# The main rows of w_in by four GpSimd transfers over 128 partitions per group, in place of four SP transfers over 32

## The chip, the core and the metric

One Trainium2 chip, one of its cores. The metric is device time in microseconds (us); lower is better. PE is TensorE, PEld its weight load, DVE VectorE, ACT ScalarE, POOL GpSimd, SP SyncE. SP computes nothing here and issues most DMA transfers. POOL computes and issues some too: those of a queue of its own, called the software queue (q0 of the profile), while SP's go out on q1.

## The reference, cut to what matters

An mLSTM cell runs over a sequence, and its output goes through a feed-forward block with an `h * cos(h)` gate.

```python
batch, n_heads, seq, head_dim = (4, 8, 768, 40)
for t in range(S):
    m_new = np.maximum(f_gate[:, :, t] + m, i_gate[:, :, t])
    f_stab = np.exp(f_gate[:, :, t] + m - m_new)
    i_stab = np.exp(i_gate[:, :, t] - m_new)
    C = f_stab[..., None, None] * C + i_stab[..., None, None] * np.einsum('bhd,bhe->bhde', vt, kt)
    n = f_stab[:, :, None] * n + i_stab[:, :, None] * kt
    h_tilde = np.einsum('bhde,bhe->bhd', C, qt)
    denom = np.maximum(np.abs(np.einsum('bhd,bhd->bh', n, qt)[:, :, None]), 1.0)
    y[:, :, t] = sigmoid(o_gate[:, :, t]) * h_tilde / denom
...
x = y.transpose(0, 2, 1, 3).reshape(3072, 320)
h = x @ w_in                   # w_in  320 x 2048, float64
return (h * np.cos(h)) @ w_out # w_out 2048 x 320, float64
```

The two weight matrices come as 8-byte floats. The kernel reads them as pairs of 32-bit integers and makes 4-byte floats of them on the chip.

## The kernel before, in words

**Tiling.** The sequence is cut into 6 chunks of 128 steps; with 4 batches that makes 24 cells (n = 4 * chunk + batch). A cell builds scores of one chunk (`scores`, PE), weighs them with decay factors (`decay_exponents`, `decay`, `weigh`), multiplies by v (`values`), normalizes and turns the result into x transposed. Cells 0 to 3 are computed first (`first_cells`); from then on the feed-forward of chunk c runs on PE between the pieces of the cells of chunk c + 1. `first_period` is the first of these periods, with cell 4; `both_parts` are the others.

**Feed-forward.** `Up(c, f2)` multiplies 256 of the 2048 columns of w_in into two PSUM banks `pup` (lines 644 and 650); `near`, `rest`, `sin` and `gate` (lines 658 to 670, ACT and DVE in turn) make the gated tile `g`; `down` multiplies by w_out (line 682). The two `pup` banks are free again when `gate` has read them.

**Weights.** w_in has 320 rows, 40 for each of 8 heads. Of each head 32 rows are "main" rows, 8 are "low" rows. The main rows lie in `w_in_sb` as [128 partitions, 2, 2048]: partition 32a + d, index i, for row d of head 2a + i. The low rows lie in `w_in_l`. Both come in four groups f of 512 columns. `weights_in(f)` issues the transfers of a group and returns three pieces: main i = 0, main i = 1, and the low one. `weights_out(p)` issues one transfer for 256 rows of w_out, eight in all. Raw words land in tiles called `bits` and `low`; a piece is then made into floats by `take_apart` (two ACT instructions, lines 148 and 150), `bound` (two on DVE, 154 and 155) and `put_together` (one on DVE, 161, one on POOL, 162). Where the calls stand decides the place in each engine's order, since the program is scheduled by hand: every engine runs its instructions in the order in which the program writes them.

**Transfers of a group.** Four of SP, one for each a: 32 partitions, 2 rows of 4 KB for each, 256 KB. Then four more of SP for the low rows, 64 KB each. `bits` of w_in has two buffers, shared with the decay tile of cell 3.

**Order around the change.** In `first_cells`: SP loads for cells 2 and 3, then `weights_in(0)` (line 866), then loads for cells 4 and 5, w_out piece 0 (907), `weights_in(1)` (926), loads of E and o, w_out pieces 1 and 2 (945, 947), `weights_in(2)` (955). At the end of `first_period`: w_out piece 3, `weights_in(3)` (1022), w_out piece 4. POOL meanwhile masks decay tiles (line 392), multiplies k by weights (411), and does line 162; it issues DMAs at lines 223, 249, 262 and, for x of each later cell, 607. The first group's pieces are used at lines 922 to 942, the second's at 988 to 1004, w_out pieces 0 and 1 at 986 and 1006, `sigmoid(1)` and `decay(5)` follow at 1007 and 1008.

Of the kernel before, what the change touches and what calls it, by code (L numbers as in the profile page):

```python
# [12 lines left out]
I32 = mybir.dt.int32  # L13
# [16 lines left out]
def kernel(  # L30
# [20 lines left out]
    nc = tc.nc  # L51

    B, H, S, D = q.shape
# [3 lines left out]
    HP = H // 2  # L57
# [6 lines left out]
    NK = DM // 128  # L64
# [66 lines left out]

    WP, WQ = 512, 2 * DM
    w_out_bits = moe_w_out.bitcast(I32).rearrange("r (n two) -> r n two", two=2)
    w_in_heads = moe_w_in.bitcast(I32).rearrange("(a e d) m -> a d e m", e=NK, d=D)

    def to_float32(*made):
        for dst, bits in made:
            take_apart(dst, bits)
        for dst, bits in made:
            bound(dst)  # L140
        for dst, bits in made:
            put_together(dst, bits)

    def take_apart(dst, bits):
        n = dst.shape[1]
        hi, lo = bits[:, 0:n, 1], bits[:, 0:n, 0].bitcast(U32)

        nc.scalar.activation(out=dst, in_=hi.bitcast(FP), func=AF.Abs)

        nc.scalar.activation(out=bits[:, 0:n, 0], in_=lo, func=AF.Copy, scale=2.0 ** -29)  # L150

    def bound(dst):
        t = dst.bitcast(I32)
        nc.vector.tensor_scalar(out=dst, in0=dst, scalar1=LEAST, scalar2=GREATEST, op0=OP.max, op1=OP.min)
        nc.vector.tensor_scalar(out=t, in0=t, scalar1=5, scalar2=2, op0=OP.logical_shift_left,
                                op1=OP.logical_shift_right)

    def put_together(dst, bits):
        n = dst.shape[1]
        hi, t, m = bits[:, 0:n, 1], dst.bitcast(I32), bits[:, 0:n, 0]  # L160
        nc.vector.scalar_tensor_tensor(out=t, in0=hi, scalar=TOP2, in1=t, op0=OP.bitwise_and, op1=OP.bitwise_or)
        nc.gpsimd.tensor_tensor(out=t, in0=t, in1=m, op=OP.add)  # L162
# [3 lines left out]

    def weights_in(f):
        bits = pb.tile([128, NK, WP, 2], I32, name="bits", tag="bits")
        for a in range(HP):
            nc.sync.dma_start(out=bits[32 * a:32 * a + 32].rearrange("r i n two -> r i (n two)"),  # L170
                              in_=w_in_heads[a, 0:32, :, ts(f, 2 * WP)])
        low = p2.tile([128, 2 * 128, 2], I32, name="low", tag="S")
        for e in range(2):
            for a in range(2):
                nc.sync.dma_start(out=low[64 * e:64 * e + 64, ts(a, 128)].rearrange("r n two -> r (n two)"), in_=w_in_last[e, 2 * f + a])
        return [(w_in_sb[:, i, ts(f, WP)], bits[:, i]) for i in range(NK)] + [(w_in_l[:, ts(f, 2)].rearrange("p a n -> p (a n)"), low)]
# [80 lines left out]
    def gates_exp():  # L257
        for e in (eG, eW):
            nc.scalar.activation(out=e, in_=e, func=AF.Exp)
        dst = G_d.rearrange("(c j q) s -> j q c s", c=R, j=2)  # L260
        for j in range(2):
            nc.gpsimd.dma_start(out=dst[j], in_=eG[j:BH:2])
# [165 lines left out]
    def turn(n):  # L428

        pool, tag = psum(n)  # L430
        pts[n] = []
        for src in (qs(n), ks(n)):
            pt = pool.tile([128, HP, C], FP, name="pt", tag=tag)
            for p in range(HP):
                nc.tensor.transpose(pt[:, p], pair(src, p), ident)
            pts[n].append(pt)
        qkT[n] = [p1.tile([128, HP, C], FP, name=f"t{i}", tag=f"t{i}") for i in range(2)]
# [396 lines left out]
    def first_cells():  # L834
        nc.vector.memset(nil, 0.0)
        gates_in()
        nc.scalar.copy(out=ident_b, in_=ident)
        load(0, "qk")
        later_gates_in()
        load(0, "v")  # L840
        load(1, "qk")
        load_o(0, (0, 1))
        load(1, "v")
        load(2, "qk")
        load_E(0)
        load_E(1)
        warm(12)
        wall_in(0, 0, pmu)
        wall_in(0, 1, psum_o())
        gates_first()  # L850
        gates_first_out()
        spread(0, 0)
        decay_exponents_half(0, 0)
        turn(0)
        turn_out(0, False)
        gates_sums()
        spread(0, 1)
        decay_exponents_half(0, 1)
        decay(0)
        weigh_k(0)  # L860
        load_E(2)
        load(2, "v")
        load_E(3)
        load_o(0, (2, 3))
        load(3)
        pieces.extend(weights_in(0))
        wall_in(1, 0, psum_o())
        wall_in(1, 1, psum_o())
        gates_less_sums()
        spread(1, 0)  # L870
        decay_exponents_half(1, 0)
        scores(0)
        gates_maxima()
        turn(1)
        weigh(0)
        sigmoid(0, slice(0, 2))
        turn_out(1, False)
        spread(1, 1)
        decay_exponents_half(1, 1)
        gates_exponents()  # L880
        decay(1)
        weigh_k(1)
        values(0)
        normalize(0)
        scores(1)
        gates_exp()
        turn(2)
        turn_out(2, False)
        warm(2)
        seam(0)  # L890
        weigh(1)
        seam_out(0)
        state(0)
        load_two(B, "qk")
        decay_exponents(2)
        gates_diagonal()
        decay(2)
        weigh_k(2)
        values(1)
        load_E(B)  # L900
        normalize(1)
        scores(2)
        turn(3)
        sigmoid(0, slice(2, 4))
        seam(1)
        load_two(B, "Kv")
        outs.append((0, weights_out(0)))
        weigh(2)
        decay_exponents(3)
        turn_out(3)  # L910
        seam_out(1)
        values(2)
        decay(3)
        weigh_k(3)
        state(1)
        normalize(2)
        warm(2)
        scores(3)
        warm(1)
        seam(2)  # L920
        weigh(3)
        take_apart(*pieces[0])
        bound(pieces[0][0])
        put_together(*pieces.pop(0))
        values(3)
        pieces.extend(weights_in(1))
        seam_out(2)
        state(2)
        for piece in pieces[0:2]:
            take_apart(*piece)  # L930
        warm(3)
        pg = gates_turn()
        normalize(3)
        gates_keep(*pg)
        bound(pieces[0][0])
        put_together(*pieces.pop(0))
        warm(2)
        seam(3)
        seam_out(3)
        decay_exponents(B)  # L940
        bound(pieces[0][0])
        put_together(*pieces.pop(0))
        load_E(B + 1)
        load_o(1)
        outs.append((1, weights_out(1)))
        load_E(B + 2)
        outs.append((2, weights_out(2)))
        low_dimensions(B)
        turn_blocks(B)
        state(3)  # L950
        decay(B)
        weigh_k(B)
        odd_values(B)
        scale_q(B)
        ahead.append(weights_in(2))

    spot = const.tile([1, 1], FP, name="spot")
    nc.gpsimd.memset(spot, 0.0)
# [11 lines left out]
    def first_period():  # L970
        n = B
        up = Up(0, 0)
        scores(n)
        warm(8, psum_o())
        for e in range(2):
            up.near(e)
        weigh(n)
        for e in range(2):
            up.rest(e)
        clear_low()  # L980
        for e in range(2):
            up.sin(e)
            up.gate(e)
        values(n)
        seam(n)
        to_float32(outs.pop(0)[1])
        up = Up(0, 1)
        take_apart(*pieces[0])
        take_apart(*pieces[1])
        bound(pieces[0][0])  # L990
        put_together(*pieces[0])
        decay_exponents(n + 1)
        for e in range(2):
            up.near(e)
        for e in range(2):
            up.rest(e)
        take_apart(*pieces[2])
        bound(pieces[1][0])
        put_together(*pieces[1])
        for e in range(2):  # L1000
            up.sin(e)
            up.gate(e)
        bound(pieces[2][0])
        put_together(*pieces[2])
        pieces.clear()
        to_float32(outs.pop(0)[1])
        sigmoid(1)
        decay(n + 1)
        state(n)
        normalize_turned(n)  # L1010
        low_out(n)
        fade(n)
        turn_blocks(n + 1)
        scale_q(n + 1)
        weigh_k(n + 1)
        sin_next()
        down(0, 0)
        pieces.extend(ahead.pop(0))
        load_two((n + 3) // 2 * 2)
        load_E(n + 3)  # L1020
        outs.append((3, weights_out(3)))
        ahead.append(weights_in(3))
        outs.append((4, weights_out(4)))
# [102 lines left out]
    pieces, outs, ahead = [], [], []  # L1126
# [41 lines left out]
```

## Time and profile before

| | us |
|---|---|
| median of 3 runs | 534.6 (534.35 to 534.88) |
| the profiled execution | 531.87 |
| its span, first to last instruction | 530.1 |
| PE busy | 512.8 (97%) |
| DVE, ACT, POOL busy | 406.9, 286.6, 247.9 |
| w_in main transfers (line 170) | 16 of 256 KB, median 7.6 from issue to landing |
| w_out transfers (line 181) | 8 of 640 KB, 5.8 |
| x transfers of POOL (line 607) | 40 of 32 KB, 3.9 |
| q1, SP's queue | 55.64 MB of 57.81 MB |
| q0, POOL's queue | 1.49 MB |

Busy time is time in which an engine had an instruction under way. A timeline row gives start, length, engine, line, operation, tiles and in square brackets the idle time before it with the instruction that ended it. A row of the chain of waits gives start, length and the work, each step being what released the next one. A row of a table by stage gives the stretch and its length, then busy time and count of PE, PEld, DVE, ACT, POOL, then the granted share of PE's clock, the busy share of the 16 DMA engines, and GB/s.

### The profile page before, as it was taken

What the parts mean: (1) busy time and instruction counts of PE and PEld (TensorE: products, weight loads), DVE (VectorE), ACT (ScalarE), POOL (GpSimd) and SP (SyncE); (2) the same over time, 40 slices, a digit from 0 to 9 for tenths busy, and PEclk for the clock granted to TensorE, in tenths of its full rate; (3) what the DMA queues carried; (4) which work ended last, traced back from release to release, by engine and by line L of the source; (5) the groups of instructions that cost most, each with busy time, mean ns of one, the idle gap of its engine ahead of it and who ended that gap; (6) DMA issues with size and microseconds to landing.
All of it is one profiled execution on the core that took longest, in us unless ns stands there. A gap on an engine that the chain in (4) does not pass through costs nothing.

```text
span 530.1 us, 10427 instructions
## 1 busy us (share of the span) xinstructions
PE 512.8 (97%) x3848; PEld 346.9 (65%) x3848; DVE 406.9 (77%) x828; ACT 286.6 (54%) x546; POOL 247.9 (47%) x409
## 2 busy tenths in 40 slices
PE   7999779999999999999999999999999999999996
PEld 3875354556657666676677677677667676666765
DVE  4896798997778878888778888868898878664636
ACT  2896797857556537744547635537735531312221
POOL 7536454673775684554454554453433333121211
PEclk9999879999999999999999999999999999999999
DMA  9999999999339259149159149159110000000001
GB/s 139 227 183 213 231 195 231 246 238 208 48 118 196 56 109 181 41 120 170 56 116 157 42 113 176 49 116 160 47 56 6 1 6 6 26 25 1 1 0 50
DMA packets 97762, 57.81 MB, mean 109 GB/s; under 512 B 62048, under 2 KB 89792, under 8 KB 97712
## 3 DMA queue, kind: packets, MB, share of 16 engines
q1 hardware_dynamic: 96240, 55.64, 51.1%
q0 software_dynamic: 1424, 1.49, 1.4%
q8 instruction: 30, 0.49, 0.4%
q14 instruction: 20, 0.16, 0.1%
q10 hardware_dynamic: 48, 0.02, 0.0%
HBM read 51.71 MB, written 4.11 MB: 105 GB/s over the span
## 4 chain that ended last, share of the span: by engine, by line
PE 81%; DVE 7%; DMA 6%; POOL 1%; issue 1%; SPq 1%; ACT 1%; DVEq 0%; POOLq 0%
PE pup L650 26%; PE acc L760 25%; PE pup L644 8%; PE ps L475 4%; PE po L682 3%; PE late L760 3%; DMA bits<-in_moe_w_in_dram 3%; PE vt L510 2%; PE vt L501 2%; PE pu L601 2%; DMA o<-in_o_gate_dram 1%; PE pw L832 1%; DVE t L456 1%; PE ph L491 1%; DMA bits<-in_moe_w_out_dram 1%
## 5 line engine op out<-in xcount | busy, mean ns | idle before, releaser
L650 PE MATMUL pup<-xT,w_in_sb 128*128 128x512 f32 x384 | 176.7, 603 | 3.1 <-DVE g L670 2.9
L658 ACT ACTIVATE n<-pup 128x512 int32<-128x512 f32 x96 | 54.0, 595 | 193.6 <-PE pup L644 141.6
L650 PEld LDWEIGHTS pup<-xT,w_in_sb 128*128 128x128 f32 x384 | 70.4, 191 | 90.3 <-issue 88.0
L661 DVE SCALAR_TENSOR_TENSOR n<-pup,n 128x512 f32<-128x512 f32 x96 | 63.0, 687 | 82.3 <-ACT n L658 80.9
L724 POOL TENSOR_TENSOR D<-g 128x128 f32<-128x128 f32 x40 | 19.7, 492 | 145.6 <-DVE g L670 145.6
L666 ACT ACTIVATE n<-n 128x512 f32<-128x512 f32 x96 | 59.3, 631 | 16.1 <-DVE n L661 16.1
L670 DVE SCALAR_TENSOR_TENSOR g<-pup,n 128x512 f32<-128x512 f32 x96 | 61.9, 684 | 2.2 <-ACT n L666 1.4
L760 PE MATMUL acc<-w_out_sb,g 128*128 128x160 f32 x320 | 58.6, 304 | 0.0
L760 PE MATMUL acc<-T,g 128*128 128x160 f32 x320 | 58.0, 301 | 0.1
L644 PE MATMUL pup<-xL,w_in_l 64*128 64x512 f32 x192 | 55.2, 650 | 0.9 <-POOL w_in_l L162 0.9
L607 POOL DMA_DIRECT2D xL<-xT x40 | 22.5, 563 | 65.1 <-DVE xT L538 61.6
L760 PEld LDWEIGHTS acc<-w_out_sb,g 128*128 128x128 f32 x320 | 47.8, 190 | 5.6 <-issue 4.2
L760 PEld LDWEIGHTS acc<-T,g 128*128 128x128 f32 x320 | 48.1, 190 | 3.7 <-issue 3.0
L406 ACT ACTIVATE E<-E,tab 128x128 f32<-128x128 f32 x160 | 49.0, 389 | 0.2
L682 PE MATMUL po<-w_out_sb,g 128*128 128x320 f32 x128 | 36.2, 436 | 0.0
L760 PE MATMUL acc<-T,S 128*128 128x160 f32 x160 | 35.0, 300 | 0.0
L475 PEld LDWEIGHTS ps<-t,t 40*128 40x128 f32 (+1 forms) x384 | 24.2, 187 | 12.6 <-DVE t L456 7.5
L682 PEld LDWEIGHTS po<-w_out_sb,g 128*128 128x128 f32 x128 | 24.0, 190 | 11.9 <-issue 1.9
L481 DVE TENSOR_TENSOR E<-ps,E 128x512 f32<-128x512 f32 x48 | 30.7, 680 | 1.4 <-PE ps L475 1.3
L644 PEld LDWEIGHTS pup<-xL,w_in_l 64*128 64x128 f32 x192 | 14.8, 187 | 24.0 <-issue 19.6
L760 PE MATMUL acc<-w_out_sb,S 128*128 128x160 f32 x160 | 28.8, 299 | 0.0
L962 ACT ACT_TABLE_LOAD x22 | 28.2, 1283 | 0.4
(178 smaller groups left out, 878.0 us busy)
## 6 DMA issues: line engine op xcount, KB each, us to landing
E<-M_d SPq DMA_DIRECT2D x22, 512.0 KB, 4.3
qr<-in_q_dram SPq DMA_DIRECT2D x36, 160.0 KB, 3.1
kr<-in_k_dram SPq DMA_DIRECT2D x36, 160.0 KB, 5.4
G<-G_d SPq DMA_DIRECT2D x20, 256.0 KB, 5.2
bits<-in_moe_w_out_dram SPq DMA_DIRECT2D x8, 640.0 KB, 5.8
bits<-in_moe_w_in_dram SPq DMA_DIRECT2D x16, 256.0 KB, 7.6
out_dram<-o_sb SPq DMA_DIRECT2D x24, 160.0 KB, 1.9
ks<-in_k_dram SPq DMA_DIRECT2D x10, 320.0 KB, 7.5
```

What stands on the lines that cost most here:

```text
L406: nc.scalar.activation(out=Es[n][:, h], in_=Es[n][:, h], func=AF.Exp, scale=-1.0, bias=tab[:, c, 0, g:g + 1])
L475: nc.tensor.matmul(ps[j][:, p], kT[r, p], qT[r, p], start=True, stop=True)
L481: nc.vector.tensor_tensor(out=w, in0=pss[n][j], in1=w, op=OP.mult)
L644: nc.tensor.matmul(pu, w_in_l[r, f2], xL[c][r].rearrange("p b t -> p (b t)"), start=ahead, stop=not ahead)
L650: nc.tensor.matmul(pu.rearrange("p (b t) -> p b t", b=B), w_in_sb[:, i, ts(2 * f2 + e, 128)], xT[c][:, i:NK * B:NK], start=(i == 0 and not ...
L658: nc.scalar.activation(out=self.n[e], in_=self.pu[e], func=AF.Copy, bias=0.25)
L661: nc.vector.scalar_tensor_tensor(out=self.n[e].bitcast(FP), in0=self.pu[e], scalar=0.25, in1=self.n[e], op0=OP.add, op1=OP.subtract)
L666: nc.scalar.activation(out=r, in_=r, func=AF.Sin, scale=TWO_PI_DOWN)
L670: nc.vector.scalar_tensor_tensor(out=g, in0=self.pu[e], scalar=TWO_PI, in1=self.n[e].bitcast(FP), op0=OP.mult, op1=OP.mult)
L682: nc.tensor.matmul(po[c][b], gs[c, f][:, ts(b, C)], w_out_sb[:, f], start=(f == 0), stop=(f == NF - 1))
L760: nc.tensor.matmul(a, lhs, rhs, start=start, stop=stop)
L962: nc.scalar.activation(out=spot, in_=spot, func=AF.Sin)
```

## The change

The main rows of a group are issued by POOL, and cut another way: one transfer for each index i and each half x of the 512 columns, over all 128 partitions, 2 KB for each, again 256 KB. The source is viewed as [i][a][d][column], so that a transfer walks four heads of 32 rows. The low rows stay on SP. Two calls of `weights_in` move with all their eight transfers: that of group 0 goes behind `gates_exp()` (which ends with two DMAs of POOL), that of group 2 from the end of `first_cells` into `first_period`, behind the making of w_out piece 0. Groups 1 and 3 stay where they were.

```diff
-    w_in_heads = moe_w_in.bitcast(I32).rearrange("(a e d) m -> a d e m", e=NK, d=D)
+    w_in_heads = moe_w_in.bitcast(I32).rearrange("(a e d) m -> e a d m", e=NK, d=D)
...
         bits = pb.tile([128, NK, WP, 2], I32, name="bits", tag="bits")
-        for a in range(HP):
-            nc.sync.dma_start(out=bits[32 * a:32 * a + 32].rearrange("r i n two -> r i (n two)"),
-                              in_=w_in_heads[a, 0:32, :, ts(f, 2 * WP)])
+        for i in range(NK):
+            for x in range(2):
+                nc.gpsimd.dma_start(out=bits[:, i, ts(x, WP // 2)].rearrange("r n two -> r (n two)"),
+                                    in_=w_in_heads[i, :, 0:32, ts(2 * f + x, WP)])
...
         load(3)
-        pieces.extend(weights_in(0))
         wall_in(1, 0, psum_o())
...
         gates_exp()
+        pieces.extend(weights_in(0))
         turn(2)
...
         scale_q(B)
-        ahead.append(weights_in(2))
...
         to_float32(outs.pop(0)[1])
+        ahead.append(weights_in(2))
         up = Up(0, 1)
```

## The prediction

> **What bounds the kernel now.** I read the slices of the page first, then PE's timeline, then the chain of waits between 42 and 76 us, then the tables by stage.
>
> ```profile
> PE   7999779999999999999999999999999999999996
> PEclk9999879999999999999999999999999999999999
> DMA  9999999999339259149159149159110000000001
> 60.54 5.34 PE L650 MATMUL pup<-xT,w_in_sb 128*128 128x512 f32 x8 [2.89 <-DVE g L670]
> 75.32 0.65 PE L501 MATMUL vt<-E,vs 128*32 128x128 f32 x8 [2.79 <-DVE E L481]
> ```
>
> PE is full but for slices 5 and 6 (53 to 80 us), where its clock drops as well; the DMA engines are full for 12 slices. So a transfer can move the end only before about 80 us; behind that PE runs nearly without a gap, and what it has gained or lost there reaches the end whole. PE's two holes there, 2.89 and 2.79 us, are the only long ones past the start. The table by stage has what they cost:
>
> ```profile
> 44.00:46.00 2.00, 2.00 (x18) 1.03 (x14) 1.34 (x3) 1.81 (x3) 2.00 (x4) 1.00 1.04 362
> 46.00:49.00 3.00, 3.00 (x77) 2.33 (x76) 2.89 (x5) 2.42 (x4) 2.01 (x2) 1.00 1.03 214
> 60.50:63.90 3.40, 3.36 (x4) 1.51 (x5) 2.78 (x6) 2.02 (x3) 1.46 (x2) 0.50 1.00 289
> 75.30:80.90 5.60, 5.58 (x76) 3.95 (x76) 5.46 (x10) 5.57 (x13) 2.85 (x3) 0.50 1.31 164
> ```
>
> After each hole PE runs at half clock (0.50), for 3.4 and 5.6 us, which costs 1.7 and 2.8 us more. The upper two rows serve below: 44 to 46 us is w_out traffic over 128 partitions, 362 GB/s; 46 to 49 us is w_in over 32 partitions, 214 GB/s, with the DMA engines equally busy (1.04, 1.03). The chain says what ends last:
>
> ```profile
> 42.95 6.57 DMA bits<-in_moe_w_in_dram
> ...
> 49.54 7.59 DMA o<-in_o_gate_dram
> ...
> 57.15 4.69 DMA bits<-in_moe_w_out_dram
> ...
> 61.86 0.79 ACT w_out_sb L148
> ...
> 75.32 0.65 PE vt L501 x8
> ```
>
> SP's transfers follow each other: group 1 of w_in, the o gate, w_out piece 1. ACT stands in order before the last, and from its start (61.86) a chain of ACT and DVE work (w_out piece 1, sigmoid, decay of cell 5, `near`, `weigh`) leads to PE's values of cell 5 (75.32): 13.46 us with hardly a gap. The earlier hole comes from ACT too:
>
> ```profile
> 53.53 0.66 ACT L148 ACTIVATE w_in_sb<-bits 128x512 f32<-128x512 f32 x1 [4.33 <-DMA bits<-in_moe_w_in_dram]
> ```
>
> ACT waits 4.33 us for group 1, so `near`, `rest`, `sin` and `gate` of Up(0, 1) are late, and PE waits for the PSUM banks.
>
> **Part 1: what POOL pays.** Each group costs POOL four issues. POOL's nearest rows:
>
> ```profile
> L607 POOL DMA_DIRECT2D xL<-xT x40: 545/565/634, 69.5 to 444.5; - x40
> L249 POOL DMA_DIRECT2D M_d<-kr x1: 645/645/645, 17.0 to 17.0; - x1
> 21.63 1.11 POOL L262 DMA_DIRECT2D G_d<-kr  x2
> 24.17 1.09 POOL L392 TENSOR_SCALAR_AFFINE_SELECT E<-E 128x1024 f32<-128x1024 f32 x1 [1.43 <-DVE E L391]
> 25.30 1.06 ACT L402 ACTIVATE E<-E 128x1024 f32<-128x1024 f32 x1 [0.89 <-POOL E L392]
> ```
>
> 64 rows take 0.565, 160 rows 0.645 us; for 128 rows I take 0.6, so 2.4 us for a group (bounds 0.545 and, as the one copy that shares POOL's time with DVE at its worst, line 162's 1.75, that is 2.2 to 7.0).
> Group 0: POOL is free of G_d at 22.74 and issues until 25.15; the mask of cell 2 behind it starts 0.97 us later than 24.17, since 1.43 of the 2.4 was idle. ACT's decay of cell 2 had waited for that mask, so it is 0.97 later, then sigmoid, copies and the decay of cell 3; `weigh(3)` on DVE and PE's values of cell 3 (33.08) come 0.8 later.
> Group 1: behind line 162 of piece 0, at 36.9 to 39.3 with that 0.8 in it; the next POOL work waits for DVE until 39.0, so 0.3 us late, and PE reaches the second half of Up(0, 0) at 41.1, when it is made (40.6). Nothing.
> Group 2: at about 53.0 to 55.4, behind line 162 of w_out piece 0; piece 0 of group 1 is then put together by 56.7, and PE wants it at 58.5. Nothing; without that cover each 0.1 us per issue would cost 0.4.
> Group 3: before the mask of cell 6 (74.39), which ACT reads at 78.36. Nothing.
>
> **Part 2: what SP and the DMA engines get.** SP loses 16 issues (0.43 us each in the median) and goes on at once to what stood behind. The bytes stay. A group is 1.05 MB: 4.9 us at 214 GB/s, 2.9 at 362. The first is the row of the old shape (4 KB in 32 partitions), the second that of w_out (2560 B in 128), nearest to the new one; I take the second, so 2.0 us saved per group, bounds 0 and 2.0. No row shows a big transfer of POOL's beside SP's; the small xL took 1.7 to 8.1 us to land, in the busy stages like SP's own, so I let both queues share in order of issue.
> Group 0 lands near 32 (ACT takes it at 33.3 now). Group 1 is issued 4 to 6 us earlier than SP's 42.55; it and w_out piece 0 are both in by 48 to 50, where ACT wants them at 48.5 and 50.0. The 4.33 us are gone. The loads of k and v for cell 4 share the engines with it, which can hold PE's values of cell 4 back by up to 1.5 us (46.3 before); that is absorbed below.
>
> **Part 3: the sum.** Without the wait, with 0.8 of shift, ACT is through `sin` of Up(0, 1) at 57.0; the gate's first bank is free about 58.3, PE finishes `down(0, 0)` at 58.5. The first hole and its half clock go: Up(0, 2) ends at 63.1 and not 66.9. But the second chain then decides: values of cell 5 start 13.46 us after ACT begins w_out piece 1, so the gain is 61.86 less the later of 57.0 and that landing. The landing was at 61.84. To its credit: two groups of w_in faster (4.0, bounds 0 and 4.0), and some 1 us of engine time lost between 53 and 59, where the eight o transfers crept out (DMA share 0.84 there). To its debit: group 2, issued from 53 now, where SP issued it at 60.0, behind that piece: 0 to 4.9, I take half of 2.9. So 61.84 - 4.0 - 1.0 + 1.5 = 58.4, bounds 57.0 and 65.7. Gain 61.86 - 58.4 = 3.4 us, PE's shift of 0.8 contained in it. The second hole and its half clock stay, since PE is early and waits for the same chain. Against the profiled execution 531.87 (span 530.1 and 1.8 around it) that is 528.5; the median stands 2.7 above that execution, so 534.6 - 3.4 = **531.2 us**. With the landing between 57.0 and 60.7 it is 529.8 to 533.5.
>
> A rule that speaks against the change: the rows
>
> ```profile
> 84.22 1.15 POOL L607 DMA_DIRECT2D xL<-xT  x2 [2.71 <-DVE xT L538]
> 84.29 0.43 DVE L155 TENSOR_SCALAR w_in_sb<-w_in_sb 128x512 int32<-128x512 int32 x1
> ```
>
> show two issues of POOL in 1.15 us while DVE ran its quick 0.43 us form. The Trainium skill (SBUF — State Buffer, "SBUF: two separate sides") holds that such a DVE instruction locks GpSimd out of writing descriptors and names 0.62 us becoming 3.1. By that figure a group would take 12.4 us and the kernel about 540 us; these rows do not agree with it.
>
> **Rivals.**
> *Second hole gone too.* If PE's hole before cell 5's values (about 2.5 us) no longer drops the clock, 2.8 more: 528.4. For: the first hole's half clock began only after nearly all of 57.5 to 60.5 was idle. Against: the second dropped it with 2.79. Chance 0.12.
> *Cancelled.* The new shape is no faster (214 GB/s) and the chain gets its piece at 61.84 - 1 + 1.5, so 62.3: 535.0. For: the engines are busy either way. Chance 0.13.
> *Slower, in the DMA queue.* Group 2 goes wholly ahead of w_out piece 1 at the old rate: 61.84 - 1.0 + 4.9 = 65.7, 3.9 us late, 538.5. It decides from the point where what group 2 takes exceeds what groups 0 and 1 save. For: the piece is SP's ninth to tenth behind low rows and o. Against: SP reaches it sooner. Chance 0.13.
> *Slower, on POOL.* An issue over 1.8 us each: then 4 x 1.8 - 1.43 = 5.8 us of shift takes ACT past 61.86, and more counts in full; at 2.5 us each 3 us, 537.6. Against: 44 issues between 0.53 and 0.66. Chance 0.07.
> *Few engines.* The new transfer lands late because it runs on a part of the 16 DMA engines. If all four of a group share 4 engines, 128 packets follow each other on each; at the software queue's 0.138 us (median of its 2 KB packets) 17.7 us, group 0 lands at 43 and ACT stands from 33.3: 10 us, 545. For: the source has 4 outermost rows. Against: POOL's transfers here all landed on 16. Chance 0.07.
> The Trainium skill (DMA: Bandwidth & Descriptors, "Why a DMA increments its semaphore by 16 and not by 1") gives that rule: the slowest dimension of both sides sets the engines, so 4 here, and for GpSimd a rotating start, under which the four transfers would fill 16 and nothing be lost. No run so far shows it.
>
> **From cases to numbers.** Forecast 0.48, then as given. Faster (forecast's, and the second hole) 0.59; within 0.2%, about 1.1 us and what a measurement here can tell, 0.14; slower 0.27. Range 528.2 to 538.5: all but the tails of the first and the dearest cases.
>
> **What would show it.** POOL's four issues near 0.6 us each; the mask of cell 2 at 25.1; no wait of ACT for `bits` at 50; PE's hole before Up(0, 2) gone and its clock whole from 60 to 64; ACT's line 148 of w_out piece 1 near 58.4 and values of cell 5 near 71.9. GB/s while w_in flows tells the shape's worth. I am wrong if w_out piece 1 lands after 61.8, if ACT waits at 33 for group 0, or if POOL blocks.

## The result, and the profile after

The changed kernel takes 542.04 us (median of 4 runs, 541.34 to 542.95) beside 534.48 us for the kernel before on the same chip: ratio 1.0152, interval 1.0134 to 1.017. It is slower, by 8.1 us with this ratio; 531.2 was forecast. The profiled execution is the one of 541.34 us, its span 539.5 against 530.1.

The slices of the page, PE, its clock and the DMA engines, 13.5 us to a slice:

```profile
PE   7996969799999999999999999999999999999995
PEclk9999979999999999999999999999999999999998
DMA  9899999799626637429338329349220000000001
bits<-in_moe_w_in_dram POOLq DMA_DIRECT2D x16, 256.0 KB, 10.4
```

PE's fourth, sixth and eighth digits (40.5 to 54, 67 to 81 and 94 to 108 us) are lower than their neighbours, the clock falls in the sixth, and behind the eighth PE is as full as before. The last line is from the table of DMA issues: a transfer of the new kind needs 10.4 us in the median from issue to landing; SP's needed 7.6. The timelines of POOL, PE with one line of DVE, and ACT show what was lost (start, length, engine, line, what, in brackets the idle time before it and what ended that):

```profile
21.93 2.76 POOL L171 DMA_DIRECT2D bits<-in_moe_w_in_dram  x4
24.70 1.10 POOL L393 TENSOR_SCALAR_AFFINE_SELECT E<-E 128x1024 f32<-128x1024 f32 x1
36.73 2.98 POOL L171 DMA_DIRECT2D bits<-in_moe_w_in_dram  x4
50.54 0.31 POOL L418 COPY vr<-vs 128x128 f32<-128x128 f32 x1 [5.02 <-DMA vs<-in_v_dram]
57.75 2.71 POOL L171 DMA_DIRECT2D bits<-in_moe_w_in_dram  x4
82.00 3.03 POOL L171 DMA_DIRECT2D bits<-in_moe_w_in_dram  x4
```

```profile
50.62 0.43 PE L502 MATMUL vt<-E,vs 128*32 128x128 f32 x8 [2.92 <-DMA vs<-in_v_dram]
64.79 3.67 PE L651 MATMUL pup<-xT,w_in_sb 128*128 128x512 f32 x8
74.20 7.11 PE L683 MATMUL po<-w_out_sb,g 128*128 128x320 f32 x16 [4.68 <-POOL w_out_sb L162]
83.33 0.43 PE L502 MATMUL vt<-E,vs 128*32 128x128 f32 x8 [0.94 <-DVE E L482]
97.44 3.67 PE L651 MATMUL pup<-xT,w_in_sb 128*128 128x512 f32 x8 [2.19 <-DVE g L671]
85.36 1.26 DVE L155 TENSOR_SCALAR w_out_sb<-w_out_sb 128x640 int32<-128x640 int32 x1
```

```profile
52.70 0.81 ACT L148 ACTIVATE w_out_sb<-bits 128x640 f32<-128x640 f32 x1 [3.56 <-DMA bits<-in_moe_w_out_dram]
54.09 0.67 ACT L148 ACTIVATE w_in_sb<-bits 128x512 f32<-128x512 f32 x1
69.76 0.78 ACT L148 ACTIVATE w_out_sb<-bits 128x640 f32<-128x640 f32 x1 [7.10 <-DMA bits<-in_moe_w_out_dram]
```

The two waits that the change removes are gone: ACT no longer waits for group 1 of w_in (second line of the last fence, 4.33 us before), and Up(0, 2) begins behind `down(0, 0)` without a hole (second line of PE's). But Up(0, 2) begins at 64.79 where it began at 60.54, and three waits are new or longer, all for transfers of **SP**: v of cell 4 (PE and POOL, 50.5), w_out piece 0 (52.70), w_out piece 1 (69.76; 7.10 us, before 3.28).

Values of cell 5 begin at 83.33 instead of 75.32, 8.0 us late, as does the weighing on DVE that they wait for. PE's wait there is short (0.94 us, before 2.79), and PE runs at full clock behind it, so that its next multiplication of main rows into `pup` begins only 5.5 us late (86.60, before 81.14). That is lost again on DVE: its lines 154 and 155 behind the weighing take 1.1 us longer (the last one 1.26 us, before 0.50), while POOL, idle there before, issues group 3 and masks. PE then waits 2.19 us for the gate at 97.44. Values of cell 6 begin at 109.37 instead of 100.20, 9.2 of the 9.4 us by which the span grew. The loads of cells 6 and 7 are late too (v lands at 89.95, before at 82.22), but the trace shows no wait for them.

The chain of waits between 15 and 90 us names the same (start, length):

```profile
38.35 1.98 SPq L346
40.39 8.58 SPq L182
...
58.64 11.11 DMA bits<-in_moe_w_out_dram
69.76 0.05 ACT w_out_sb L148
83.33 0.43 PE vt L502 x8
```

SP itself stood for 8.58 us in the issue of w_out piece 0 (2.11 before), behind v's load, so its whole queue is late. Then piece 1, issued at 58.64 (57.15 before), flies for 11.11 us (4.69 before). The share of the two queues while v should have come, 42 to 45 us, first in the changed kernel, then in the kernel before (packets, MB, share of 16 engines):

```profile
q0 software_dynamic: 292, 0.56, 102.7%
q14 instruction: 1, 0.01, 1.0%
q1 hardware_dynamic: 1, 0.00, 0.1%
```

```profile
q1 hardware_dynamic: 1339, 0.69, 98.7%
```

q0 is POOL's queue, q1 SP's. For 3 us the engines serve only group 1; SP's queue moves one packet. In the trace v's packets begin at 45, though SP was through with issuing them at 40.34, and v lands at 50.49 instead of 44.09.

### The profile page after: what moved, and what is told of

Read it like the earlier page. It is cut to its first block, busy times and chain, and to the rows that moved or that the text cites. A ratio compares the mean times of both kernels' runs of the same rounds, so it can differ in the third digit from the quotient of the medians.

```text
span 539.5 us, 10425 instructions
## 1 busy us (share of the span) xinstructions
PE 513.3 (95%) x3848; PEld 346.5 (64%) x3848; DVE 412.4 (76%) x828; ACT 286.4 (53%) x546; POOL 259.5 (48%) x425
## 4 chain that ended last, share of the span: by engine, by line
PE 77%; DMA 6%; DVE 6%; SPq 4%; ACT 4%; issue 1%; POOL 1%; DVEq 0%; ACTq 0%
PE pup L651 25%; PE acc L761 24%; PE pup L645 8%; PE ps L476 3%; PE po L683 3%; PE late L761 3%; PE vt L511 2%; DMA bits<-in_moe_w_out_dram 2%; PE vt L502 2%; DMA low<-in_moe_w_in_dram 2%; SPq L182 2%; PE pu L602 1%; DMA E<-M_d 1%; DVE t L457 1%; PE pw L833 1%
## 5 line engine op out<-in xcount | busy, mean ns | idle before, releaser
L683 PE MATMUL po<-w_out_sb,g 128*128 128x320 f32 x128 | 38.8, 459 | 5.1 <-POOL w_out_sb L162 5.1
L683 PEld LDWEIGHTS po<-w_out_sb,g 128*128 128x128 f32 x128 | 25.4, 202 | 18.4 <-POOL w_out_sb L162 6.7
L645 PEld LDWEIGHTS pup<-xL,w_in_l 64*128 64x128 f32 x192 | 14.4, 184 | 25.0 <-issue 19.6
## 6 DMA issues: line engine op xcount, KB each, us to landing
bits<-in_moe_w_in_dram POOLq DMA_DIRECT2D x16, 256.0 KB, 10.4
```

The costliest lines, as they stand in the source:

```text
L645: nc.tensor.matmul(pu, w_in_l[r, f2], xL[c][r].rearrange("p b t -> p (b t)"), start=ahead, stop=not ahead)
L683: nc.tensor.matmul(po[c][b], gs[c, f][:, ts(b, C)], w_out_sb[:, f], start=(f == 0), stop=(f == NF - 1))
```

## The experiments

Three theories were told apart. **Few engines**: the cut is what costs, because a transfer of the new shape keeps its data on a part of the DMA engines. **Collision**: any second queue that carries a megabyte takes the engines away from SP's transfers, which are due earlier. **POOL**: the issues cost POOL's own time. Some expectations call them A, B and C. Besides, the forecast's gain itself was tested. Ratios are to the kernel before on the same chip.

| run | w_in's main rows | median us | ratio (interval) |
|---|---|---|---|
| e1_pool_rows32 | all by POOL, old cut | 539.44 | 1.0111 (1.0063 to 1.0159) |
| e4_g2_sp | group 2 by SP | 540.81 | 1.0112 (1.0064 to 1.0161) |
| e5_g12_sp | groups 1, 2 by SP | 539.48 | 1.0099 (1.0064 to 1.0134) |
| e8_swap | kernel before, w_out piece 1 a little earlier | 534.6 | 1.0002 (0.9978 to 1.0026) |
| e6_g0_only | group 0 by POOL | 532.61 | 0.9991 (0.9974 to 1.0008) |
| e6_g1_only | group 1 by POOL | 539.03 | 1.0122 (1.0103 to 1.0141) |
| e6_g2_only | group 2 by POOL | 542.9 | 1.018 (1.0154 to 1.0205) |
| e6_g3_only | group 3 by POOL | 537.84 | 1.0089 (1.0064 to 1.0114) |
| e7_late | all by POOL, issued later | 551.42 | 1.0359 (1.0326 to 1.0393) |
| e2_sp_cols | all by SP, new cut | 554.73 | 1.0411 (1.0387 to 1.0434) |
| e10_words | by SP; POOL issues words | 534.0 | 1.0017 (1.0002 to 1.0033) |
| e9_early | kernel before, w_out piece 1 much earlier | 533.53 | 0.9998 (0.9983 to 1.0013) |

**The queue without the cut.** The changed kernel with the old view of w_in and

```diff
-        for i in range(NK):
-            for x in range(2):
-                nc.gpsimd.dma_start(out=bits[:, i, ts(x, WP // 2)].rearrange("r n two -> r (n two)"),
-                                    in_=w_in_heads[i, :, 0:32, ts(2 * f + x, WP)])
+        for a in range(HP):
+            nc.gpsimd.dma_start(out=bits[32 * a:32 * a + 32].rearrange("r i n two -> r i (n two)"),
+                                in_=w_in_heads[a, 0:32, :, ts(f, 2 * WP)])
```

> POOL still issues four transfers per group at the changed kernel's places, but in the old cut: 32 partitions, 2 rows of 4 KB each, so that the outermost dimension of both sides is 32. Theory A (few engines: the changed cut puts each transfer's data on 4 of the 16 DMA engines, and SP's transfers, which need all 16, wait for those): the group spreads over 16 engines, lands within some 6 us of its issue in the middle stages, w_out piece 1 lands by 62 us and not at 69.74, and the time comes back to 532 to 536 us. Theory B (any second queue with this traffic takes the engines from SP's, whatever the cut): w_out piece 1 still lands at 68 to 70 us and the time stays at 540 to 543. Theory C (POOL's own time, 2.7 to 3.0 us per group): 540 to 543 as well, with the landings early.

Measured: 1.0111. SP's issue of w_out piece 0, PE at its values of cell 4, and ACT at w_out piece 1:

```profile
40.70 9.28 SPq L181 DMA_DIRECT2D bits<-in_moe_w_out_dram  x1
52.20 0.66 PE L501 MATMUL vt<-E,vs 128*32 128x128 f32 x8 [5.25 <-DMA vs<-in_v_dram]
66.45 0.81 ACT L148 ACTIVATE w_out_sb<-bits 128x640 f32<-128x640 f32 x1 [2.51 <-DMA bits<-in_moe_w_out_dram]
```

v of cell 4 lands at 52.06, later than in the changed kernel: the collision is there without the new cut. Piece 1 flies for 6.65 us, not 11.1, and lands at 66.43, between the 62 of theory A and the 68 to 70 of theory B; the time lies between theirs as well. So the cut is part of what group 2 does to piece 1. As times the two kernels can't be told apart, their intervals overlap.

**The cut without the queue.** The changed kernel with one word changed back:

```diff
-                nc.gpsimd.dma_start(out=bits[:, i, ts(x, WP // 2)].rearrange("r n two -> r (n two)"),
+                nc.sync.dma_start(out=bits[:, i, ts(x, WP // 2)].rearrange("r n two -> r (n two)"),
```

> The new cut (four transfers over 128 partitions a group) at the changed kernel's places, but issued by SP: one queue, in order. If the cut is what costs (few-engines theory), group 1 lands later than the 53.43 of the kernel before, or the transfers behind it do, and the time is 539 to 543 as in the changed kernel. If the second queue is what costs (collision theory), k and v of cell 4 land by 44 and w_out piece 1 by 63, as before, and the time is 533 to 537; up to 537 because a transfer whose data lies on four engines keeps the transfers behind it on those engines waiting.

Measured: 1.0411, the slowest of all, outside what either theory gave. Two stretches of it in which such a group flows, by windows (window, its length, busy time of PE, PEld, DVE, ACT, POOL, then granted clock, share of the DMA engines, GB/s):

```profile
25.00:28.00 3.00, 3.00 (x48) 2.65 (x47) 2.90 (x9) 2.95 (x4) 0.74 (x1) 1.00 0.27 94
53.00:56.00 3.00, 3.00 (x69) 1.98 (x62) 2.84 (x5) 1.51 (x2) 1.98 (x2) 1.00 0.26 89
```

A quarter of the engines is busy and 89 to 94 GB/s flow, where the old shape had all of them and 214. The four transfers of group 0 land one after another, at 28.06, 31.14, 34.99 and 38.32. So on SP's queue the few-engines theory holds in full; and as the cut alone costs so much there, this run does not tell what the second queue costs. By POOL the same shape was not so slow: group 0 of the changed kernel lands at 28.39, 30.24, 32.23 and 33.52, and its queue alone moved 205 GB/s at 27 us.

**Group by group.** One group by POOL in the new cut, the others by SP in the old cut, all at the changed kernel's places (here for group 1):

```diff
+        if f != 1:
+            for a in range(HP):
+                nc.sync.dma_start(out=bits[32 * a:32 * a + 32].rearrange("r i n two -> r i (n two)"),
+                                  in_=w_in_rows[a, 0:32, :, ts(f, 2 * WP)])
+        else:
+            for i in range(NK):
...
```

> Group 0 alone by POOL in the new cut, at the changed kernel's place. Here SP's queue has only the 160-byte loads and small ones beside it, and nothing of the trace of the changed kernel up to 36 us is late. Collision theory and POOL theory both: 533 to 536 (at most 1.3 us for the mask of cell 2). If it gives over 537, the start has a price that the traces do not show.

> Group 1 alone goes by POOL in the new cut, at the place of the changed kernel; the others go by SP in the old cut at that kernel's places. Collision theory: v of cell 4 lands 4 to 7 us later than the 44.09 of the kernel before, w_out piece 1 is issued 1 to 2 us later and lands near 63 with its short flight of about 4.5 us, values of cell 5 near 77 (before 75.32), and the time is 1.5 to 3 us over the kernel before. Few-engines theory (the cut is what costs): the same delay, because this run has the cut, so it does not tell them apart; POOL theory: 2.7 to 3.0 us of POOL's time for four issues, which shows as a wait for POOL somewhere between 37 and 50 us, and the time is up to 3 us over with v of cell 4 landing as before.

> Group 2 alone by POOL in the new cut, at the place of the changed kernel. Up to 57 us this is the kernel before. Collision theory: w_out piece 1 is issued near 57.2 and lands 8 to 11 us later (66 to 68) where before it took 4.7 us, values of cell 5 begin near 80 to 82, and the time is 3 to 6 us over the kernel before, the largest of the three single groups. If the first hole of the tensor engine going away were worth its time, as predicted, the time would be 3 us under.

> Group 3 alone by POOL in the new cut, at the place of the changed kernel. Up to 75 us this is the kernel before. Collision theory: v and k of cells 6 and 7 land some 7 us later than the 82.22 of the kernel before, holes ahead of the values of cells 6 and 7, and the time is 1.5 to 5 us over. The run with groups 0 and 3 by POOL gave 5.5 us over, so if groups 0 and 3 are told apart this run gives near 5 and group 0 near nothing; if it gives under 2, group 0 has a price that the trace did not show.

Group 0 costs nothing that can be measured, each of the others alone 0.9 to 1.8%: 6.5, 9.6 and 4.7 us for groups 1, 2 and 3 by these ratios. For groups 1 and 2 that is more than the 1.5 to 3 and 3 to 6 us expected. SP's issues and PE with group 1 alone, then with group 2 alone, then PE with group 3 alone:

```profile
33.82 8.01 SPq L352 DMA_DIRECT2D vs<-in_v_dram  x1
41.89 10.19 SPq L188 DMA_DIRECT2D bits<-in_moe_w_out_dram  x1
53.61 0.65 PE L508 MATMUL vt<-E,vs 128*32 128x128 f32 x8 [6.89 <-DMA vs<-in_v_dram]
80.81 0.43 PE L508 MATMUL vt<-E,vs 128*32 128x128 f32 x8 [2.03 <-DVE E L488]
```

```profile
59.30 0.68 SPq L188 DMA_DIRECT2D bits<-in_moe_w_out_dram  x1
74.75 7.47 PE L689 MATMUL po<-w_out_sb,g 128*128 128x320 f32 x16 [5.85 <-POOL w_out_sb L163]
84.25 0.43 PE L508 MATMUL vt<-E,vs 128*32 128x128 f32 x8 [0.94 <-DVE E L488]
```

```profile
95.83 2.08 PE L651 MATMUL pup<-xL,w_in_l 64*128 64x512 f32 x4 [3.73 <-POOL w_in_l L163]
```

Each group hits the SP transfer that was in flight or next when it was issued. Group 1 hits v of cell 4 (and here, issued at 35.67 and not 36.73, k as well: it lands at 52.17, in the changed kernel at 44.32): values of cell 5 at 80.81, 5.5 us late. Group 2 hits w_out piece 1 (issued at 59.30, landed at 70.28, 11.0 us): 84.25, 8.9 us late. Group 3 hits k and v of cells 6 and 7 (v at 88.67), but nothing waits long for them. SP stands 7.40 us in v's issue (2.79 before) and issues w_out piece 3 only at 86.37; ACT waits 2.33 us for it, and the work on w_in's low rows, behind it in DVE's order, is what PE waits for at 95.83. The four ratios add up to 3.8%, the changed kernel has 1.5%: the prices don't add. As the traces read, group 1 caught v but not k in the changed kernel, and where SP's and POOL's later issues all came late together, group 2's delay took the place of group 1's (8.0 us at values of cell 5, where the two alone make 14.4); no run tests that apart.

**Two mixtures.** Group 2 by SP in the old cut and at the place of the kernel before, the rest as changed; the second run has `f in (1, 2)` in the first line:

```diff
+        if f == 2:
+            for a in range(HP):
+                nc.sync.dma_start(out=bits[32 * a:32 * a + 32].rearrange("r i n two -> r i (n two)"),
+                                  in_=w_in_rows[a, 0:32, :, ts(f, 2 * WP)])
+        else:
...
         scale_q(B)
+        ahead.append(weights_in(2))
...
         to_float32(outs.pop(0)[1])
-        ahead.append(weights_in(2))
```

> The changed kernel, but group 2 by SP in the old cut and at its old place; groups 0, 1 and 3 by POOL in the new cut. Theories A and B: w_out piece 1 has the engines for itself again and lands some 5 us after its issue near 58.6, at about 63.5 and not at 69.74; values of cell 5 start near 77 and not 83.3; 535 to 537 us. Theory C: only one of POOL's four groups is saved, 540 to 542.

> As the run before, but group 1 by SP in the old cut too; only groups 0 and 3 by POOL. Theories A and B: v of cell 4 lands near 44 to 46 and not at 50.5, the two holes of PE at its values of cell 4 (2.9 and 1.1 us) are gone, and the time is 533 to 536 us. Theory C: half of POOL's cost stays, 537 to 539.

Group 2 taken back brings little (1.0112 for 1.0152, with intervals that overlap), though the ACT wait for piece 1 is gone. The 535 to 537 us of theories A and B were missed, and the 540.81 us lie in the range of theory C, which the run with the issues alone (below) refutes. The trace has the reason: v of cell 4 is worse off here (PE waits 7.98 us), SP stands 11.10 us in the issue of w_out piece 0, and values of cell 5 begin at 82.76, not near 77. With groups 1 and 2 taken back the first 75 us are those of the kernel before (values of cell 5 at 75.47), and the time is still 1.0% over: that was not expected (533 to 536). PE's later holes (1.92, and 4.13 us at 97.77, for the work on w_in's low rows) and SP's 7.94 us in the issue of v at 76.50 put it on group 3, and the run with group 3 alone confirmed it.

**The issues without the bytes.** SP issues all as in the kernel before, and POOL, at the changed kernel's places:

```diff
+        for a in range(HP):
+            nc.gpsimd.dma_start(out=none[:, HP * f + a:HP * f + a + 1], in_=w_in_word[0:128, HP * f + a:HP * f + a + 1])
```

> SP issues all of w_in in the old cut, in the order of the kernel before; at the changed kernel's four places POOL issues four transfers of 4 bytes in each of 128 partitions into a tile that nobody reads. POOL pays its issues (about 0.7 us each, 2.7 to 3.0 us a group) and moves next to nothing (2 KB a transfer). POOL theory: the issues themselves cost, so the time is 538 to 543. Collision theory: only the bytes cost, so 533 to 536.

Measured: 1.0017 (1.0002 to 1.0033), some 0.9 us. (A transfer moves 128 words, 512 B; the 2 KB are those of a group.) An issue of this kind takes 0.54 us, 2.17 a group, so 0.5 to 0.9 us of the 2.7 to 3.0 us that a group costs POOL in the changed kernel is not in it. POOL's time is not what makes 1.5%. Nor are the new places: SP issues from them in the old order and at nearly the old times (v of cell 4 at 33.70, before 33.63; w_out piece 1 at 57.50, before 57.15).

**The same groups, issued later.** Low rows on SP as changed; the main transfers of group 1 behind the copy that waits for v of cell 4, of group 2 behind the work on w_out piece 1, of group 3 behind the copy that waits for v of cell 6:

```diff
-        pieces.extend(weights_in(1))
+        low = low_in(1)
...
         odd_values(B)
+        pieces.extend(weights_in(1, low))
         scale_q(B)
```

> All four groups by POOL in the new cut, with as many issues as in the changed kernel and SP's queue issuing the same transfers in the same order; only the place of the main issues on POOL is moved: group 1 behind the copy that waits for v of cell 4, group 2 behind the arithmetic on w_out piece 1, group 3 behind the copy that waits for v of cell 6. Collision theory: v of cell 4 lands near 44, w_out piece 1 near 62 (group 1's tail may hold it to 63), v of cells 6 and 7 near 82, and the time is 533 to 537. POOL theory and few-engines theory: as many issues and the same cut, so 540 to 543 as in the changed kernel. If the late groups themselves come too late for their arithmetic, a wait for bits from w_in's dram ahead of the activation of groups 1, 2 or 3 shows it.

Measured: 551.42, far outside the 533 to 537, and outside the 540 to 543 of the other theories. ACT's and PE's waits in it:

```profile
61.45 0.69 ACT L148 ACTIVATE w_in_sb<-bits 128x512 f32<-128x512 f32 x1 [10.66 <-DMA bits<-in_moe_w_in_dram]
115.74 0.66 ACT L148 ACTIVATE w_in_sb<-bits 128x512 f32<-128x512 f32 x1 [9.13 <-DMA bits<-in_moe_w_in_dram]
```

```profile
47.92 0.43 PE L505 MATMUL vt<-E,vs 128*32 128x128 f32 x8
51.15 0.66 PE L514 MATMUL vt<-qG,st 128*32 128x128 f32 x8 [2.80 <-POOL qG L464]
```

What the collision theory said of SP's transfers holds in part: v of cell 4 lands at 46.51 and PE doesn't wait for it; piece 1 flies for 7.3 us; v of cells 6 and 7 lands only at 88.41, beside the tail of group 2. But the groups now come too late: group 1 needs 12 to 15 us from issue to landing beside the o gate's transfers, and ACT waits 10.66 us for it, for group 3 9.13. And four issues put in front of the making of qG cost PE 2.80 us. So group 1 stands between two due times, v of cell 4 before it and its own at 54, and behind v there is no room for a flight of 12 us.

**The gain without the queue.** Two runs of the kernel before with w_out piece 1 issued earlier by SP, one place (in front of `load_o(1)`) and right behind group 1:

```diff
         pieces.extend(weights_in(1))
+        outs.append((1, weights_out(1)))
...
         load_o(1)
-        outs.append((1, weights_out(1)))
```

> The kernel before, with w_out piece 1 issued ahead of the eight o-gate transfers in place of behind them. If the 13.46 us chain from ACT's start on that piece sets the end of this stage, the piece lands near 58.6 in place of 61.84, the o gate near 62 (ACT reads it about 1.5 us after its work on the piece), and 1.5 to 3.3 us are gained: 531 to 533 us. If the o gate comes too late instead, no gain: 534 to 536.

> The kernel before with one transfer moved in SP's order: w_out piece 1 is issued right behind group 1 of w_in, some 9 us earlier. The prediction's gain term without its queue: the activation on w_out piece 1, which waited 3.28 us until 61.86, begins by 58.7, and if the gain were 61.86 less the later of 57.0 and the landing, values of cell 5 begin near 72 and the time is 530 to 532. Rival: that wait covers another one close behind (the run with piece 1 one place earlier began the activation at 60.65 and gained nothing), so values of cell 5 begin at 74 or later and the time is 533 to 535.

Measured: no gain in either (1.0002, 0.9998). ACT's wait for piece 1 is 1.93 us in the first run and gone in the second. DVE's timeline of the kernel before, then ACT, DVE and PE of the second run:

```profile
61.41 0.30 DVE L155 TENSOR_SCALAR w_in_l<-w_in_l 128x256 int32<-128x256 int32 x1
62.68 0.71 DVE L154 TENSOR_SCALAR w_out_sb<-w_out_sb 128x640 f32<-128x640 f32 x1 [0.52 <-ACT w_out_sb L148]
71.90 1.29 DVE L661 SCALAR_TENSOR_TENSOR n<-pup,n 128x512 f32<-128x512 f32 x2 [0.76 <-ACT n L658]
74.50 1.28 DVE L481 TENSOR_TENSOR E<-ps,E 128x512 f32<-128x512 f32 x2
```

```profile
59.01 0.78 ACT L148 ACTIVATE w_out_sb<-bits 128x640 f32<-128x640 f32 x1
61.70 1.25 DVE L155 TENSOR_SCALAR w_in_l<-w_in_l 128x256 int32<-128x256 int32 x1
63.32 0.49 DVE L154 TENSOR_SCALAR w_out_sb<-w_out_sb 128x640 f32<-128x640 f32 x1
74.45 1.28 DVE L481 TENSOR_TENSOR E<-ps,E 128x512 f32<-128x512 f32 x2
55.11 6.27 PE L682 MATMUL po<-w_out_sb,g 128*128 128x320 f32 x16 [2.24 <-POOL w_out_sb L162]
75.28 0.43 PE L501 MATMUL vt<-E,vs 128*32 128x128 f32 x8 [2.03 <-DVE E L481]
```

ACT begins piece 1 at 59.01, 2.85 us earlier and without waiting. PE's hole before Up(0, 2) has only moved: PE waits 2.24 us at 55.11 for w_out piece 0, and Up(0, 2) begins at 61.22 (before 60.54). And the weighing of cell 5, the instruction that PE waits for, begins on DVE at 74.45 where it began at 74.50. DVE is the reason: in the kernel before it was idle for only 0.52 us on account of piece 1, since it still had the rest of group 1 to do, and for 0.76 us at 71.90, for `near` at the end of the chain that ACT begins with piece 1. In the second run both are gone, and lost again: lines 154 and 155 for group 1's low piece and for w_out piece 1 took 1.45 us longer in all (one line 155 took 1.25 us in place of 0.30, while POOL ran line 162 beside it from 61.48 to 62.79).

## Why the prediction was wrong

Right: the structure. Both waits that the change was to remove are gone, and in the changed kernel piece 1's landing decides: values of cell 5 begin 13.57 us after ACT starts on it, where 13.46 was forecast. What POOL pays was nearly right: 2.7 to 3.0 us a group for 2.4 (0.68 to 0.73 us in most issues for 0.6). The mask of cell 2 comes at 24.70 (25.1 forecast), PE's values of cell 3 at 33.15 (before 33.08), and group 0 is in by 33.52 with no wait of ACT; alone it costs nothing. "Nothing" for groups 1 and 3 holds less well: the issues push POOL's line 162 and masks beside DVE's line 155, which takes 2.94 us at 39.28 (before 1.06) and 1.26 us at 85.36 (before 0.50). PE waits 0.57 and 0.55 us for POOL in Up(0, 0), which the wait for v then covers; the second delay shows in PE's wait at 97.44.

Wrong, **what bounds the kernel**: "So a transfer can move the end only before about 80 us". Group 3 alone costs 0.9%, by transfers that land behind 80 us. And the DMA digits shown are full for the first ten slices, to 132 us, not for twelve.

Wrong, **Part 2**: "so I let both queues share in order of issue". SP had begun the issue of v of cell 4 before POOL's group 1 (34.23, 36.73), but v's packets began only at 45, when some two thirds of group 1 had been moved. So k and v did not cost PE "up to 1.5 us": v landed 6.4 us late, PE's values of cell 4 began at 50.62 for 46.29, and nothing absorbed it, since SP stood in its own issues meanwhile. POOL in turn waited 5.02 us for v, and group 2 was issued from 57.75, not 53, two of its four transfers ahead of piece 1 (58.64).

Wrong, the landing of piece 1: 61.84 - 4.0 - 1.0 + 1.5 = 58.4, with bounds 57.0 and 65.7. It was 69.74, beyond the upper one. The credit of 4.0 for a shape that flows as w_out does did not come: by SP the shape flowed at 89 to 94 GB/s, not 362, and in the changed kernel beside piece 1 (60 to 69 us) POOL's queue moved some 60 GB/s, its four transfers landing one by one at 64.55, 71.69, 75.33 and 78.84. The debit for group 2, 1.5, at most 4.9, came out at 6.4 (a flight of 11.1 us for 4.7), and SP reached piece 1 1.5 us later, not sooner. The bound of 4.9 took a group for a block that goes ahead once; it went beside piece 1 for the whole flight.

Wrong, **Part 3**: "the gain is 61.86 less the later of 57.0 and that landing". The row with ACT's wait was read as the chain, and DVE's rows behind it were not: its 0.52 us of idle time, and 0.76 us for `near`, were the most that piece 1 alone could bring. Piece 1 brought forward by SP gave nothing. Group 1 coming earlier as well, which the forecast also had, could have moved DVE's own work; no run had that without the collision.

The rivals: "slower, in the DMA queue" was the right place with too small a price, 3.9 us for 8.0 at values of cell 5; its condition, group 2 wholly ahead of piece 1, was not met, since group 2 flowed beside piece 1 and landed until 78.84. "Second hole gone too" counted PE's half clock as time to be won. In the run with group 0 alone that hole (1.65 us) no longer drops the clock, and values of cell 6 begin at 100.67, before at 100.20: nothing was won, as DVE's gate is waited for behind it (2.16 us at 88.74). "Few engines" was right about the shape and wrong about where it shows: not at group 0, but in group 2's flight and, in full, by SP. The Trainium skill (DMA: Bandwidth & Descriptors, "Why a DMA increments its semaphore by 16 and not by 1") has the slowest dimension set the engines, 4 here; the DMA share of 0.26 to 0.27 in the run with the new cut by SP agrees. Its rotating start for GpSimd agrees with group 0 (205 GB/s), and group 2 landing piece by piece does not show it. "Slower, on POOL" is refuted by the words of e10_words; the rule of the Trainium skill weighed there (SBUF — State Buffer, "SBUF: two separate sides") would have had issues of 3.1 us, and none of the sixteen took more than 0.96.

Not settled: by what rule an engine takes group 1's packets ahead of v's; the trace doesn't name the engine of a packet. Nor why DVE's lines 154 and 155 take longer beside POOL's work. Not tried: the later places in the old cut, and group 1 issued ahead of v by SP itself, which would part the second queue from the earlier issue. No run is shown to beat the kernel before.

## What to carry to other kernels

Here one queue kept transfers in the order in which they were due; a second one that carried a megabyte a group did not, and what it delayed was whatever the first queue had in flight or came to next, with all that was queued behind it. Before moving a load to another issuer, list the first queue's transfers that are in flight at its new issue time with their due times, and price the load at its whole flight, not at its bytes. And before a wait on one engine is counted as gain, read the idle time of the next engine in the chain: 3.28 us on ACT were 0.52 on DVE, and 0.76 more further down.

## What was not expected of the hardware

- A load of 160-byte pieces held the issuing queue: SP stood 6.11 us in v's issue (6.59 in the kernel before) and, with group 1 in the engines, 8.58 us in the next (11.10 in one run). Without group 1 the next took 2.11 us.
- Four transfers of 256 KB over 128 partitions, from four heads of 32 rows, flowed at 89 to 94 GB/s by SP, with a quarter of the engines; over 32 partitions at 214 GB/s with all. By POOL the same four reached 205 GB/s beside small loads and some 60 GB/s beside a transfer of SP's over 128 partitions.
- Prices of single groups (−0.1, 1.2, 1.8 and 0.9%) do not add up to that of all four (1.5%). k of cell 4 landed at 44.32 where POOL's group 1 was issued 4.0 us behind it, and at 52.17 where it was issued 2.5 us behind it.
- DVE's line 155 on a group's low piece took 0.30 us with POOL idle beside it (61.41, kernel before) and 2.94 us beside line 162 and a mask of POOL (39.28, changed kernel).
